# Engine programs in the main block of a fused attention and MLP kernel, without a block of their own and the barrier behind it

## The chip, the cores and the metric

The kernel runs on one core of one Trainium2 chip. The metric is device microseconds of one execution, the median over several. Each timed execution also lists its *span*: the time from the first to the last instruction that the profile recorded. The time is longer than the span; that difference I call *the part outside the span*. Spans are listed to 0.1 us, so a mean over four to eleven runs is good to some 0.03 us.

A *semaphore* is a counter that one engine or transfer raises and for which another engine waits: in before, the store that SP issued at 143.623 us raises the one for which SP's record from 145.308 to 145.336 us waits. SP (SyncE) computes nothing here: its records in before are 52 transfers issued, 10 semaphore instructions, two drains and one branch. A *drain* is an instruction with which an engine waits for its own earlier work: VectorE's in before lasted from 143.345 to 143.950 us, past the end of its last addition at 143.898.

## The reference

```python
def reference(A_x, A_wqkv, A_wo, B_x, B_w1, B_b1, B_w2, B_b2):
    x = A_x                                    # 1 x 2048 x 448, bf16
    xn = _layernorm(x, axis=-1)
    s = _A_ref(xn, A_wqkv, A_wo)               # linear attention, 16 heads of 28, phi(q), phi(k)
    g = _silu(_B_ref(xn, B_w1, B_b1, B_w2, B_b2))   # squared-relu MLP, 448 -> 1792 -> 448
    return x + s * g
```

What it computes does not matter for this change; what matters is that the output leaves in 16 stores, the last of them very late.

## The kernel before

The kernel builds a list of operations per engine with its own scheduler, works out the semaphore waits, and then emits one program for each of the five engines. The change is in that last step:

```python
    def emit(self, nc, es):
        sems = {e: es.enter_context(nc.semaphore("q_" + e)) for e in self.ENGINES}
        # ... (cut: one semaphore for each DMA; the waits of each operation)
        block = es.enter_context(nc.Block())

        def body_of(e):
            def body(h):
                for op in self.order[e]:
                    for s, v in waits[op]:
                        h.wait_ge(s, v)
                    op.emit(h, e).then_inc(op.sem, 16 if op.nbytes else 1)
                if e == "sp":
                    for o in self.ops:
                        if o.nbytes and o.writes and o.writes[0][0] == "out":
                            h.wait_ge(o.sem, 16)        # SP waits for all 16 stores

            return body

        block.gpsimd(body_of("pool"))
        block.sync(body_of("sp"))
        block.scalar(body_of("act"))
        block.tensor(body_of("pe"))
        block.vector(body_of("dve"))
        # leaving the ExitStack closes the block: in the listing every engine branches to
        # an end block, drains, and passes a barrier of all five engines
```

The barrier in the end block works as follows: SP, ScalarE, VectorE and TensorE each drain and add one to a "gather" semaphore; GpSimd drains, waits for the four, and then adds four to a "release" semaphore, for which the others wait. In the trace of before, the drains of GpSimd, TensorE, VectorE, ScalarE and SP end at 142.697, 142.845, 143.950, 144.494 and 145.937 us, and GpSimd's two semaphore instructions follow at 145.962 and 146.040. The constructor of the program emits the same barrier at the start, behind four small memsets of constants (the last ends at 0.511 us, GpSimd's release at 0.699). That one belongs to both kernels.

## Time and profile before

| | before |
|---|---|
| time, median of 3 runs before the prediction (all) | 147.88 us (147.73 to 148.08) |
| span of the profiled run | 146.1 us |
| TensorE busy | 141.3 us, 97% |
| between 9.65 and 142.80 us | PE busy 133.07 of 133.15 us |

The head of the profile's page for before, with busy time, share and number of instructions for each engine:

```profile
span 146.1 us, 3240 instructions
## 1 busy us (share of the span) xinstructions
PE 141.3 (97%) x1330; PEld 69.2 (47%) x1330; DVE 97.2 (67%) x224; ACT 79.8 (55%) x154; POOL 21.2 (14%) x39
```

The same by stage (busy time of each engine in three stretches of the span):

```profile
0.00:9.65 9.65, 8.18 (x41) 3.27 (x42) 5.15 (x16) 4.54 (x12) 2.42 (x16) 1.00 0.80 251
9.65:142.80 133.15, 133.07 (x1289) 65.89 (x1289) 91.05 (x206) 75.26 (x143) 18.76 (x23) 1.00 0.24 58
142.80:146.20 3.40, 0.00 (x0) 0.00 (x0) 0.99 (x3) 0.00 (x0) 0.00 (x0) 0.90 0.30 101
```

The columns are the stretch and its length, then PE, PE's weight load, DVE, ACT and POOL, the granted clock, the DMA share and GB/s. For 133 us TensorE has no gap that counts (0.08 us in all), so only the 9.65 us before and the 3.3 us after can be shortened by a change that leaves the work alone.

The head, in order of time (start, length, engine, line, operation):

```profile
0.41 0.10 POOL L1109 MEMSET const-uint8-127<- 128x1 uint8 x1
0.80 0.10 POOL L350 MEMSET eps<- 128x1 f32 x1 [0.29 <-POOLq L1109]
0.81 0.40 SPq L396 DMA_DIRECT2D x_tok<-in_A_x_dram  x1
0.93 0.27 DVE L341 MEMSET junk<- 128x256 uint32 x1 [0.93 <-PEq L1109]
3.72 0.63 DVE L447 BATCH_NORM_STATS2 st<-x_tok 128x6 f32<-128x448 bf16 x1 [2.52 <-DMA x_tok<-in_A_x_dram]
```

L1109 is the line on which the program is constructed; what waits for it waits for the first barrier.

The waits of SP's queue near the end (who waited for whom: us in total, times, longest):

```profile
SPq L271 <- DMA out_dram<-obuf: 1.3, 2, 0.9
SPq L285 <- PEq L285: 0.2, 1, 0.2
```

L271 is the wait for the stores, L285 the exit of the `with` that closes the block. Semaphore instructions, branches and drains count as no engine's busy time, so the tail itself must be read from the trace's single records. For before, in us from the start of the span:

```
SP      wait for the last store (paired with another)  145.696 - 145.724
SP      branch, with one more wait on it               145.764 - 145.797
SP      drain                                          145.924 - 145.937
GpSimd  semaphore: all four have arrived               145.962 - 145.979
GpSimd  semaphore: release the four                    146.040 - 146.057
SP      released                                       146.082 - 146.099
ScalarE released                                       146.086 - 146.103
VectorE released                                       146.093 - 146.114
TensorE released                                       146.094 - 146.145   = end of the span
```

From the end of SP's last store wait to the end of the span are 0.42 us.

### The profile page before, as it was taken

The page shows a single profiled execution, that of the slowest core. Times are in us where ns is not written, and L with a number is a line of the kernel's source. Part 1 is how long each engine was busy: PE and PEld are TensorE (multiplying, and loading weights), DVE is VectorE, ACT ScalarE, POOL GpSimd, SP SyncE. Part 2 cuts the span into 40 slices and gives each one's busy share as a digit, 9 for nine tenths or more (in the row PEclk, how much of TensorE's full clock was granted, in tenths as well). Part 3 has the DMA queues.
Part 4 walks back from the last instruction along what each step waited for, and adds up shares of the span by engine and source line. Part 5 has one row for each costly group of instructions (what it writes and reads, how often), then busy time and mean ns, then how long its engine had stood idle before and what let it go on. Part 6 is the DMA issues. An engine that isn't in the chain of part 4 may idle for free.

```text
span 146.1 us, 3240 instructions
## 1 busy us (share of the span) xinstructions
PE 141.3 (97%) x1330; PEld 69.2 (47%) x1330; DVE 97.2 (67%) x224; ACT 79.8 (55%) x154; POOL 21.2 (14%) x39
## 2 busy tenths in 40 slices
PE   6999999999999999999999999999999999999990
PEld 2344446644444446443545535545555555555440
DVE  0979688888978995999995594973052341604583
ACT  3557799889887888889797191613030220301310
POOL 6000000000000000008900000000050505144140
PEclk9999999999999999999999999999999999999999
DMA  4997649995301100000000000000001011020122
GB/s 124 307 332 215 161 88 350 307 204 112 72 4 36 36 4 0 0 0 4 0 0 0 4 0 0 7 0 0 0 17 51 31 36 63 0 65 2 63 94 94
DMA packets 15513, 10.54 MB, mean 72 GB/s; under 512 B 7244, under 2 KB 15116, under 8 KB 15500
## 3 DMA queue, kind: packets, MB, share of 16 engines
q1 hardware_dynamic: 15040, 9.89, 26.5%
q10 hardware_dynamic: 460, 0.46, 0.9%
q8 instruction: 10, 0.16, 0.5%
q14 instruction: 3, 0.02, 0.1%
HBM read 6.94 MB, written 1.84 MB: 60 GB/s over the span
## 4 chain that ended last, share of the span: by engine, by line
PE 93%; DVE 3%; DMA 2%; issue 0%; DVEq 0%
PE pb L651 29%; PE pb L852 29%; PE pb L601 7%; PE pb L912 7%; PE pb L683 6%; PE pb L623 6%; DMA x_tok<-in_A_x_dram 2%; PE pb L638 1%; DVE st L447 1%; PE pb L689 1%; PE pb L830 1%; PE pb L775 1%; PE pb L741 1%; PE pb L803 1%; PE pb L930 1%; PE pb L490 1%
## 5 line engine op out<-in xcount | busy, mean ns | idle before, releaser
L651 PE MATMUL pb<-xT,w 64*128 64x512 bf16 x392 | 51.6, 376 | 0.1
L852 PE MATMUL pb<-w,r 64*128 64x448 bf16 x448 | 48.2, 349 | 0.0
L660 ACT ACTIVATE r<-pb,b1f 128x512 bf16<-128x512 f32 x56 | 35.0, 689 | 9.0 <-PE pb L651 8.9
L852 PEld LDWEIGHTS pb<-w,r 64*128 64x128 bf16 x448 | 22.8, 94 | 21.0 <-PE pb L852 0.6
L651 PEld LDWEIGHTS pb<-xT,w 64*128 64x128 bf16 x392 | 21.7, 94 | 21.7 <-ACT r L660 0.7
L870 ACT ACTIVATE gbuf<-gbuf 128x448 bf16<-128x448 bf16 x15 | 8.3, 577 | 35.7 <-DVE gbuf L860 35.7
L860 DVE TENSOR_TENSOR gbuf<-pb,b2b 128x448 bf16<-128x448 f32 x15 | 8.7, 621 | 25.4 <-PE pb L852 25.4
L899 POOL TENSOR_TENSOR obuf<-obuf,x_tok 128x448 bf16<-128x448 bf16 x12 | 12.1, 1029 | 57.4 <-DVE obuf L889 57.4
L601 PE MATMUL pb<-w_qkv,xT 64*128 64x448 bf16 (+1 forms) x106 | 16.0, 350 | 0.0
L623 PE MATMUL pb<-xT,w_qkv 64*128 64x512 bf16 x84 | 15.6, 376 | 0.0
L668 DVE TENSOR_TENSOR r<-r 128x512 bf16<-128x512 bf16 x37 | 13.7, 443 | 0.0
L912 PE MATMUL pb<-msb,pqT 64*128 64x448 bf16 x90 | 13.6, 349 | 0.0
L669 ACT ACTIVATE r<-r 128x512 bf16<-128x512 bf16 x19 | 11.3, 633 | 0.0
L447 DVE BATCH_NORM_STATS2 st<-x_tok 128x6 f32<-128x448 bf16 x16 | 9.4, 611 | 2.5 <-DMA x_tok<-in_A_x_dram 2.5
L889 DVE TENSOR_TENSOR obuf<-pb,gbuf 128x448 bf16<-128x448 f32 (+1 forms) x17 | 9.6, 593 | 2.2 <-PE pb L852 1.7
L579 ACT ACTIVATE pk<-pb 128x448 bf16<-128x448 f32 x16 | 8.1, 540 | 3.6 <-PE pb L601 2.9
L591 DVE SCALAR_TENSOR_TENSOR pk<-pb,pk 128x448 bf16<-128x448 f32 x16 | 9.8, 622 | 0.4
L378 POOL MEMSET ehd<- 128x896 bf16 x1 | 0.8, 844 | 62.9 <-DVE zb L613 62.9
L839 DVE TENSOR_TENSOR pqT<-pqT,pb 128x512 bf16<-128x512 bf16 x12 | 7.7, 684 | 3.1 <-PE pb L830 3.1
L683 PE MATMUL pb<-pk,xn 128*128 128x448 bf16 x48 | 9.6, 353 | 0.0
L601 PEld LDWEIGHTS pb<-w_qkv,xT 64*128 64x128 bf16 (+1 forms) x106 | 6.8, 94 | 5.1 <-DVE xT L500 0.4
L623 PEld LDWEIGHTS pb<-xT,w_qkv 64*128 64x128 bf16 x84 | 6.3, 94 | 4.3
(90 smaller groups left out, 117.5 us busy)
## 6 DMA issues: line engine op xcount, KB each, us to landing
out_dram<-obuf SPq DMA_DIRECT2D x15, 112.0 KB, 1.7
w<-in_B_w_dram SPq DMA_DIRECT2D x1, 1568.0 KB, 9.5
x_tok<-in_A_x_dram SPq DMA_DIRECT2D x3, 448.0 KB, 4.4
w_qkv<-in_A_wqkv_dram SPq DMA_DIRECT2D x3, 336.0 KB, 4.8
w<-in_B_w_dram SPq DMA_DIRECT2D x2, 384.0 KB, 4.6
w<-in_B_w_dram SPq DMA_DIRECT2D x1, 576.0 KB, 5.7
w_o<-in_A_wo_dram SPq DMA_DIRECT2D x1, 392.0 KB, 10.8
w_qkv<-in_A_wqkv_dram SPq DMA_DIRECT2D x6, 56.0 KB, 4.3
```

The source lines that it names most:

```text
L447: "dve", lambda e, _: e.bn_stats(st6[:, si, :], x_tok[:, si, :]), [("x", si)], [("st", si)], 0.553
L591: lambda e, _: e.scalar_tensor_tensor(out=slot, in0=ps(buf)[0:rows, 0:n], scalar=1.0 + 1e-6, in1=slot, op0=ALU.add, op1=ALU.max),
L601: return e.matmul(ps(b)[:, 0:D], xT[half[h], c, si * P : (si + 1) * P], w_qkv[half[h], c, D : 2 * D], start=start, stop=stop,)
L623: return e.matmul(ps(b)[:, 0:512], w_qkv[half[h], c, m * P : (m + 1) * P], xT[half[h], c, g * 512 : (g + 1) * 512], start=start, stop=stop,)
L651: return e.matmul(ps(b)[:, 0:512], w_1[half[h], c, fi * P : (fi + 1) * P], xT[half[h], c, g * 512 : (g + 1) * 512], start=start, stop=stop,)
L660: lambda e, _: e.activation(out=slot, in_=ps(b)[:, 0:512], func=AF.Relu, bias=b1f[:, fi : fi + 1]),
L668: return e.tensor_tensor(out=slot, in0=slot, in1=slot, op=ALU.mult)
L669: return e.activation(out=slot, in_=slot, func=AF.Square)
L683: last = e.matmul(ps(b)[:, 0:D], xn[:, si, c * P : (c + 1) * P], pk[:, si, :], start=(si == 0), stop=(si == NT - 1),)
L852: return e.matmul(ps(b)[:, 0:D], r2[half[h], fi, si * P : (si + 1) * P], w_2[half[h], fi, :], start=start, stop=stop)
L899: eng, lambda e, _: e.tensor_tensor(out=ob, in0=ob, in1=x_tok[:, si, :], op=ALU.add),
L912: return e.matmul(ps(b)[:, 0:D], q, msb[half[h], k, :], start=start, stop=stop)
```

## The change

The intent is to save the branches into and out of each engine's own block, and the barrier of all engines at the block's end. SP still waits for the stores. The whole diff:

```diff
@@ -257,7 +257,6 @@
             waits[op] = need
             prev[e] = known
             done[op] = known
-        block = es.enter_context(nc.Block())
 
         def body_of(e):
             def body(h):
@@ -272,11 +271,11 @@
 
             return body
 
-        block.gpsimd(body_of("pool"))
-        block.sync(body_of("sp"))
-        block.scalar(body_of("act"))
-        block.tensor(body_of("pe"))
-        block.vector(body_of("dve"))
+        body_of("pool")(nc.gpsimd)
+        body_of("sp")(nc.sync)
+        body_of("act")(nc.scalar)
+        body_of("pe")(nc.tensor)
+        body_of("dve")(nc.vector)
```

## The prediction

> **What bounds the kernel.** TensorE. The page of the profile gives PE 97% busy over a span of 146.1 us; the chain of work that ended last is 93% PE, 3% DVE, 2% DMA. PE runs without a break that matters from 9.65 us (first L651 matmul) to 142.8 us; the change touches nothing in these 133 us, only the ends.
>
> **What the change does.** The data instructions, their semaphores and their order on each engine stay. Two things go: (1) at the head, one unconditional branch per engine from the main block into the engine's own block; (2) at the tail, one branch per engine into the end block, and there a drain and a barrier of all five engines. The barrier at the head (waits "SPq L1109 <- PEq L1109") comes from the program's construction and stays; the one at L285 goes. SP's waits for the stores stay.
>
> **Tail, from the trace's single records.** SP's last paired semaphore wait (the last store) ends at 145.724 us. Then the branch, which also carries one wait, 145.764 to 145.797; 127 ns of nothing; SP's drain at 145.924; GpSimd's two semaphore instructions at 145.962 and 146.040; the release of the others, TensorE's ending at 146.145, the end of the span. Without these the last wait becomes a plain semaphore instruction ending at about 145.78. Saved: 146.145 - 145.78 = 0.36 us, in series behind the last store's landing, so all critical. (The other engines' drains were over by 144.5 us.)
>
> **Head.** From the first barrier's release 68 ns pass on SP and 66 ns on ACT until the first load's issue; between two semaphore waits on SP at the tail it is some 40 ns. [...] The chain begins with that issue (DMA x_tok 2.89 us, BN statistics, xn, transposes), and PE's warm-up (gated by the junk memset, 172 ns behind the barrier) moves forward too, so the gain should carry through: about 0.04 us.
>
> **Sum.** 0.36 + 0.04 = 0.40 us, 0.3% of 147.88: predicted 147.48 us.
>
> **What I don't see.** The measured time is 1.7 us longer than the span. [...] If the runtime's end is quicker when engines arrive together, some is given back; if it profits from four engines arriving early, the gain is some tenths more. The three runs of before spread over 0.35 us, as much as the effect.
>
> **Range.** 147.1 to 147.8 us (8 in 10). Faster by over 2%: 1%. Within 2%: 98%. Slower by over 2%: 1%.
>
> **What would show each step.** Tail: the span ends with an SP semaphore wait some 60 ns after that of the last store, no L285 in the waits. Head: first load issued at about 0.77 instead of 0.81 us, junk memset and first matmul likewise earlier; BN statistics and transposes move by the same. Middle: first L651 to last L932 matmul still about 133 us at the same clock. Difference of spans and of times agree within 0.15 us.
>
> **What would make it wrong.** [...]the compiler treating waits otherwise in one block than in five; the runtime's end depending on arrival order[...].

The sum came to 0.40 us: 0.36 for the tail and 0.04 for the head. The 0.36 us are worked out from the records named there; its 145.78 is the branch's start at 145.764 and the 17 ns that SP's unpaired wait at 144.007 took. Of the 0.04 us the records named give 68 - 40 = 28 ns; the rest of that term rested on a figure for a branch that no run here shows. "The runtime's end" is whatever runs in the part outside the span, and "PE's warm-up" is the row of ten junk matmuls, the first of which starts at 1.256 us, 56 ns behind the end of the junk memset.

## The result

| | before | after |
|---|---|---|
| time, median (all runs of this comparison) | 147.98 us (147.73 to 148.15, 4) | 147.08 us (146.98 to 147.13, 4) |
| span of the profiled run | 146.1 us | 145.9 us |
| end of the last store's wait to end of span | 0.42 us | 0 |
| part outside the span, mean | 1.73 us | 1.24 us |

The ratio is 0.9941, 95% interval 0.9927 to 0.9955. A ratio here is the mean time of one kernel's fast runs over that of the other's of the same rounds, so it is not quite the ratio of the medians quoted. The four runs of before in this comparison have no span, and lie within 0.3% of each other. The part outside the span of before comes from the control run c_before below (5 runs) and the 11 runs of before beside it.

The kernel gained 0.90 us, over twice the 0.40 us predicted; the median lies 0.02 us below the low end of the range.

The head of the page for after:

```profile
span 145.9 us, 3228 instructions
## 1 busy us (share of the span) xinstructions
PE 140.8 (97%) x1330; PEld 69.1 (47%) x1330; DVE 97.2 (67%) x224; ACT 79.8 (55%) x154; POOL 21.2 (15%) x39
```

The 12 instructions fewer are five drains, six semaphore instructions and one branch.

The stages of after, columns as above:

```profile
0.00:9.65 9.65, 7.73 (x41) 3.21 (x41) 5.09 (x15) 4.50 (x12) 2.42 (x16) 1.00 0.82 248
9.65:142.80 133.15, 132.96 (x1290) 65.87 (x1289) 91.09 (x207) 75.33 (x143) 18.77 (x23) 1.00 0.25 59
142.80:146.20 3.40, 0.15 (x1) 0.00 (x0) 1.03 (x4) 0.00 (x0) 0.00 (x0) 0.76 0.30 101
```

The middle is the same. The head of after, in order of time (line numbers are one lower, because a line went):

```profile
0.41 0.10 POOL L1108 MEMSET const-uint8-127<- 128x1 uint8 x1
0.80 0.10 POOL L349 MEMSET eps<- 128x1 f32 x1 [0.29 <-POOLq L1108]
0.81 0.40 SPq L395 DMA_DIRECT2D x_tok<-in_A_x_dram  x1
0.93 0.27 DVE L340 MEMSET junk<- 128x256 uint32 x1 [0.93 <-PEq L1108]
3.58 0.63 DVE L446 BATCH_NORM_STATS2 st<-x_tok 128x6 f32<-128x448 bf16 x1 [2.38 <-DMA x_tok<-in_A_x_dram]
```

The instruction starts have not moved: first load at 0.81 us, junk memset at 0.93 us, in both. On the single records, SP's release to its first load is 68 ns before and 68 ns after. The first statistics came 0.14 us earlier in this run, but on the arrival of the load, not on its issue.

The waits of SP's queue near the end of after:

```profile
SPq L395 <- DVE obuf L898: 1.4, 2, 0.9
SPq L270 <- DMA out_dram<-obuf: 1.3, 2, 0.9
```

The line of the closed block is gone, and the span ends with SP's wait for the last store (145.838 to 145.865). The last work of GpSimd is a residual addition; it is the only line of GpSimd in the last 5 us of after:

```profile
141.75 1.03 POOL L898 TENSOR_TENSOR obuf<-obuf,x_tok 128x448 bf16<-128x448 bf16 x1 [1.91 <-DVE obuf L888]
```

It ends 3.08 us before the span does. In before, GpSimd's last instruction (the release of the barrier) ended 0.09 us before the end of the span. Keep this pair in mind.

The span of this profiled pair shrank by 0.28 us and not by 0.42, because the loads came differently. The chain of waits of before starts on the first tile of x:

```profile
0.81 2.89 DMA x_tok<-in_A_x_dram
3.70 0.02 issue
3.72 0.64 DVE st L447
```

and that of after on a later tile, which landed at 5.61 us:

```profile
1.25 4.36 DMA x_tok<-in_A_x_dram
5.61 0.02 issue
5.64 0.63 DVE st L446
```

so its last TensorE group started 0.15 us later. This is scatter, not the change: the spans of before alone range from 146.0 to 146.9 us over the timed runs. The part outside the span hardly scatters, by some 0.05 us (1.68 to 1.77 us in the eleven runs of before beside c_before), and it is the better instrument.

### The profile page after: what moved, and what is told of

The parts are those of the page before. It is cut to its first block, busy times and chain, and to the rows that moved or that the text cites. A ratio compares the mean times of both kernels' runs of the same rounds, so it can differ in the third digit from the quotient of the medians.

```text
span 145.9 us, 3228 instructions
## 1 busy us (share of the span) xinstructions
PE 140.8 (97%) x1330; PEld 69.1 (47%) x1330; DVE 97.2 (67%) x224; ACT 79.8 (55%) x154; POOL 21.2 (15%) x39
## 4 chain that ended last, share of the span: by engine, by line
PE 93%; DMA 3%; DVE 2%; ACTq 0%; issue 0%; DVEq 0%
PE pb L650 29%; PE pb L851 29%; PE pb L600 7%; PE pb L911 7%; PE pb L682 6%; PE pb L622 6%; DMA x_tok<-in_A_x_dram 3%; PE pb L637 1%; PE pb L688 1%; PE pb L829 1%; PE pb L774 1%; PE pb L740 1%; PE pb L802 1%; PE pb L929 1%; PE pb L489 1%; DVE st L446 0%
```

## The experiments

All kernels gave correct results and keep the waits on the stores. The first four ran on one chip, the next four in a second call, the last four in a third, each beside its own runs of before. "Outside" is the part outside the span.

| run | time, median | ratio to before (95%) | outside, mean |
|---|---|---|---|
| c_before | 147.89 | 0.9989 (0.9972 to 1.0006) | 1.73 |
| a_barrier | 147.85 | 0.9987 (0.9967 to 1.0006) | 1.73 |
| a_allwait | 147.81 | 0.9987 (0.9970 to 1.0005) | 2.01 |
| a_drain | 147.19 | 0.9934 (0.9915 to 0.9952) | 1.26 |
| a_pool_last | 147.83 | 0.9991 (0.9973 to 1.0010) | 2.03 |
| a_act_last | 147.20 | 0.9953 (0.9936 to 0.9971) | 1.40 |
| a_pe_last | 147.22 | 0.9955 (0.9940 to 0.9970) | 1.52 |
| a_dve_last | 147.45 | 0.9967 (0.9953 to 0.9982) | 1.34 |
| d_all_but_pool | 147.41 | 0.9966 (0.9951 to 0.9981) | 1.54 |
| d_pool_early | 147.41 | 0.9968 (0.9955 to 0.9981) | 1.65 |
| d_pool_drain | 147.81 | 0.9993 (0.9980 to 1.0006) | 2.16 |
| d_before_drain | 147.75 | 0.9990 (0.9978 to 1.0002) | 1.74 |

### c_before: where does the time outside the span stand?

The kernel before, unchanged.

> Control: the kernel before, unchanged, to have its span beside its time in every timed run. Both theories: time within 0.1 us of the other runs of before (147.9), span about 146.2. The point is the part of the time outside the span: if the after kernel's gain is half outside the span, this is about 1.7 us here against about 1.25 in the runs of after (147.13 less 145.9). If it is about 1.3 here too, the gain lies inside the span, in the first microseconds and the tail.

Measured: outside 1.73 us in its five runs and 1.73 in the eleven runs of before beside it. In the two later calls before gave 1.71 and 1.74, so values of different calls can be compared to some 0.03 us. So 1.73 - 1.24 = 0.49 us of the gain lie where no record of the trace is. That is the larger half, and my prediction had no number for it.

### a_barrier: the block or the barrier?

```diff
         body_of("dve")(nc.vector)
+        nc.all_engine_barrier()
```

> After, plus one barrier of all engines (drains included) behind the last instruction, still without a block of its own. Theory B (the barrier costs everything, the block nothing): the time returns to before, ratio 0.999 to 1.001, the span's tail from the last store's wait to the end about 0.35 us, and the part outside the span rises to that of before. Theory K (the block, its label or the branch on SP costs a part): the time comes back by only some 0.3 to 0.4 us, to about 147.45, and the part outside the span stays near 1.25 us.

Measured: 147.85 us, outside 1.73. The barrier alone brings the time back to before within the interval, and the whole part outside the span. The page shows it under its own line again:

```profile
SPq L279 <- PEq L279: 0.2, 1, 0.2
```

The single records show a smaller share for the block. Here SP's store wait ends at 145.832 us, the drain follows at 145.872 and the span ends at 146.093: 0.26 us against 0.42 in before. The 0.16 us between them is the branch on SP and the hole behind it. So theory B holds for the barrier, and theory K for 0.16 us; the difference of the times (means 148.09 for before and 147.92) is too uncertain to show this by itself.

### a_allwait: late engines without a barrier

```diff
-                if e == "sp":
+                if True:
                     for o in self.ops:
```

> After, but all five engines wait for the stores themselves, so all reach the end of the program together, without drain, gather or release. Theory A (what follows the program is longer when five engines arrive late than when only SP does): time about 147.5, 0.4 above after, the span as in after, the part outside the span about 1.7 us. Rival S (what follows counts from the last engine's arrival only): time as after (147.08 within 0.1), the part outside the span about 1.25 us.

Measured: 147.81 us, outside 2.01. The span is as in after (mean 145.92, after 145.83), there is no drain, gather or release, and still the time is nearly that of before. Rival S is out: something behind the program is longer when engines other than SP are late, 2.01 us against 1.24. It went even above the 1.7 us expected.

### a_drain: the drains without the barrier

```diff
         body_of("dve")(nc.vector)
+        for h in (nc.gpsimd, nc.sync, nc.scalar, nc.tensor, nc.vector):
+            h.drain()
```

> After, plus a drain at the end of each engine, but no barrier. If the drain is what costs (rival D): SP's drain adds its 13 ns and a gap of about 0.1 us to the span's tail and something outside the span, 147.3 or more. Theories A and S: only SP's drain counts, +0.05 to +0.1 us, 147.15.

Measured: 147.19 us, outside 1.26. In the trace the span ends 0.05 us behind SP's last pair of waits, and the part outside is 0.02 us above that of after, so drains alone cost less than 0.1 us; rival D is out.

### a_pool_last, a_act_last, a_pe_last, a_dve_last: one late engine at a time

```diff
-                if e == "sp":
+                if e == "pool":     # or "act", "pe", "dve"
                     for o in self.ops:
```

> After, but GpSimd alone waits for the stores in place of SP (SP's program ends with its last store). Theory M (each engine has its own fixed end behind its last instruction, and the time ends with the last of these ends): one or more of the four engines tried has a part outside the span of 1.8 to 2.0 us, as when all five wait (2.01); GpSimd is my guess for it, time then about 147.8. Theory N (the longer end needs several engines arriving together): 1.25 us here as with SP, time about 147.1.

> The same with ScalarE alone. Theory M: its own value, from about 1.0 to 2.0 us outside the span, the largest of the five engines being that of the run in which all wait (2.01). Theory N: about 1.25 us, time about 147.1.

> The same with TensorE alone. Theory M: its own value, from about 1.0 to 2.0 us outside the span. Theory N: about 1.25 us, time about 147.1.

> The same with VectorE alone. Theory M: its own value, from about 1.0 to 2.0 us outside the span; if it or another engine is below SP's 1.25 us, that kernel is faster than after by the difference. Theory N: about 1.25 us, time about 147.1.

Measured, outside the span, by the engine that ends last: SP 1.24 us (after), VectorE 1.34, ScalarE 1.40, TensorE 1.52, GpSimd 2.03. GpSimd alone makes up what five late engines cost (2.01). Theory M holds and theory N is out. The time of a_pool_last is 147.83 us with a span like that of after, so all of after's gain outside the span, and more, is lost by letting GpSimd be the last. None of the four beats after; SP, which already waits in after, is the cheapest engine to end on.

These values hold a constant that I cannot split off (whatever lies before the first record counts too). What is shown are the differences: against SP, 0.10, 0.16, 0.28 and 0.79 us. The smallest, VectorE's, is the least certain, because SP's value comes from another call.

The time of a_dve_last (147.45 us) is above those of ScalarE and TensorE although its part outside is smaller than theirs. Its spans were longer, 146.10 us in the mean against 145.82 and 145.72. In its profiled run the stretch from TensorE's last weight load to the end of the span is as in the others (3.13 us, 3.12 in a_pe_last), so there the difference lies earlier; it was not followed further.

### d_all_but_pool and d_pool_early: does the rule predict?

```diff
# d_all_but_pool
-                if e == "sp":
+                if e != "pool":
# d_pool_early, added after SP's waits
+                if e == "pool":
+                    for o in self.ops:
+                        if o.nbytes and o.writes and o.writes[0][0] == "out" and o.eng != "act":
+                            h.wait_ge(o.sem, 16)
```

> After, but SP, ScalarE, VectorE and TensorE wait for the stores; GpSimd alone ends early. Theory M (the time is the latest over the engines of its last instruction plus that engine's own end): the part outside the span is that of TensorE, the largest of the four, 1.52 us, time about 147.25 to 147.35. If joint arrival matters by itself: near the 2.01 us of all five.

> After, with GpSimd also waiting for all the stores but the last-landing one, which lands some 0.38 us behind the last but one. SP ends the span as in after. Theory M: GpSimd ends 0.37 us before the span's end, so the part outside is 2.03 - 0.37 = 1.66 us, more than SP's own 1.24; time about 147.5. If GpSimd's long end only counts when GpSimd is the last: 1.24 us, 147.08.

Measured: 1.54 us with four late engines and GpSimd early (expected 1.52), and 1.65 us with GpSimd 0.37 us ahead of the span's end (expected 1.66). So for engines that end on waits for stores, the end of the time is the latest, over the engines, of "its last instruction plus its own end". Behind the barrier the rule holds less well, as the next run shows. By these numbers, as an estimate, GpSimd must be 2.03 - 1.24 = 0.79 us ahead of SP before its end is hidden; in after it is 3.08 us ahead.

### d_pool_drain: why 1.82 us and not 2.03 in the barrier?

With the barrier, GpSimd's last instruction is 0.09 us before the end of the span, so its own end is there 1.73 + 0.09 = 1.82 us, not 2.03. I thought of the drain that GpSimd makes early in the barrier (141.565 to 142.697 us in before).

```diff
-                if e == "sp":
+                if e == "pool":
+                    h.drain()
                     for o in self.ops:
```

> GpSimd alone waits for the stores, as in a_pool_last, but drains itself first, as it does in the barrier. In before and in a_barrier GpSimd's last instruction ends 0.09 us before the span's end, so its end there is 1.73 + 0.09 = 1.82 us, 0.2 less than the 2.03 us measured with GpSimd waiting without a drain. If the drain is what makes it shorter: 1.82 us outside the span, time about 147.6. If not: 2.03 us, 147.83, and those 0.2 us stay open.

Measured: 2.16 us, no shorter but 0.13 longer. The drain does not explain the 0.2 us. They stay open: if GpSimd sets the time behind the barrier, its own end is not quite a constant, but lies between 1.82 and 2.16 us with what it did last.

### d_before_drain: the branch on SP

Before, with the last wait of SP carried by a drain; the compiled program then has no branch there.

```diff
                         if o.nbytes and o.writes and o.writes[0][0] == "out":
                             h.wait_ge(o.sem, 16)
+                    h.drain()
```

> Before, block and barrier kept, with a drain as SP's last instruction in its block; the compiled program then has no branch at SP's tail (the last wait rides on the drain), all labels as in before. If the taken branch costs what the trace suggests (0.42 us from the last store's wait to the end of the span in before, 0.26 in a_barrier, so 0.16 us), this tail is 0.30 to 0.34 us (the extra drain costs some 0.05 back), the part outside the span stays 1.73 us, and the time is about 0.1 us below before. If labels or the block itself cost anything, the tail stays at 0.42 us.

Measured on the single records:

```
SP      wait for the last store (paired with another)  145.624 - 145.652
SP      drain, with one more wait on it                145.691 - 145.704
SP      drain of the barrier                           145.752 - 145.759
GpSimd  semaphore: all four have arrived               145.785 - 145.802
TensorE released                                       145.916 - 145.967   = end of the span
```

The tail is 0.315 us, as expected, against 0.42 in before, with all else of the block in place; outside 1.74. So the labels and the block itself cost nothing and the branch does: 0.42 - 0.315 = 0.105 us, to which the 0.06 us that the extra drain takes (from one drain to the next) must be added, 0.16 us, the same as from a_barrier. The time, ratio 0.9990 (0.9978 to 1.0002), does not resolve this 0.1 us.

## Why the prediction was right and wrong

**What bounds the kernel: right.** TensorE's 133 us are the same before and after.

**Tail in the span: right in kind, a little small.** Predicted 0.36 us, shown 0.42. The wait that had sat on the branch fell into a pair with another, so no further instruction followed the last store's wait. The runs divide the 0.42 into 0.16 for SP's branch (a COMPARE_BRANCH in the trace of before: its record takes 33 ns, then 127 ns pass until SP's drain) and 0.26 for the barrier. That the whole 0.40 us predicted comes so close to the 0.42 measured in the span is luck: the tail was put 0.06 us too low and the head, below, 0.04 us too high.

**Head: wrong.** The step "one unconditional branch per engine at the head, about 0.04 us" measured 0. The listing of the program has such branches, but the compiled one holds only labels there, and the engines run on into their block. (35 labels and one branch in before, 5 labels and no branch in after.) The one branch compiled in before is SP's at the tail, the carrier of a wait. The trace says it too: one branch record in all, and 68 ns from release to first load in both kernels. I had taken 68 against 40 ns as room for a branch, without knowing whether there was one.

**Behind the program: the term that was missing, and the step that failed.** The prediction named the question ("if it profits from four engines arriving early, the gain is some tenths more"), but the sum put 0 there. It measured 0.49 us. The reason that the runs show: each engine has its own end behind its last instruction, GpSimd's being the longest by 0.5 us and more (2.03 us against 1.24 to 1.52). The barrier makes GpSimd, whose last addition in before ended at 142.631 us, one of the last to finish (146.057 us), because it gathers and releases. Without the barrier SP ends alone, with the shortest end (1.24 us), and GpSimd's is hidden under the last store's flight (in after GpSimd's last addition ends at 142.785 us, SP's wait for that store at 145.865). That GpSimd sets the 1.73 us of before is inferred from the other runs and not tested by itself: TensorE, the next, gives 1.52 behind a wait, which is too little; but GpSimd's 2.03 less the 0.09 us by which it is ahead would give 1.94, which is 0.2 too much. For TensorE the last record is the same kind of wait in both (51 ns), while GpSimd's is a wait in a_pool_last (43 ns) and a release in before (17 ns), which speaks for GpSimd and doesn't prove it. That the barrier brings the 0.49 us, whichever engine sets them, is shown by a_barrier: it differs from after by that one line behind the program.

What runs in the part outside is not in the trace, and no run here shows what fills the 1.24 to 2.03 us. Shown are only their dependence on the engine that ends last and, by d_all_but_pool and d_pool_early, the rule of the latest engine.

**"Difference of spans and of times agree within 0.15 us": wrong.** Even the means show it: the span gives about 0.4, the time 0.9.

**The sum.** 0.42 in the span and 0.49 outside are 0.91 us; the medians differ by 0.90. Nothing else is needed. That the two agree to 0.01 us is luck, since the spans scatter by some tenths.

**Open.** Why GpSimd's end is 1.82 us behind the barrier and 2.03 to 2.16 behind a row of waits, why GpSimd's end is the longest, and whether it is GpSimd that sets the time behind the barrier. A barrier from which GpSimd leaves early, which would tell, was not run.

## What to carry to other kernels

In this kernel a barrier at the end of the program cost more than its own records (0.26 us in the span, 0.49 behind it): it makes GpSimd, whose last addition ended 3.5 us before the span did, end 0.09 us before it, and the engine with the slowest finish (GpSimd, 2.03 us) then sets the time, as inferred above. Let one engine wait for the outputs, the one with the shortest end (SP here, 1.24 us), and keep GpSimd's last instruction the better part of a microsecond ahead (0.79 us by the estimate above). When a time and the profile's span differ, track that difference run by run; here it scattered far less than either (by 0.09 us in the eleven runs of before beside c_before, whose times lay 0.74 us apart and whose spans 0.8) and showed what no record does.
